# Sixteen small loads issued by GpSimd beside a saturated load queue

## The chip, the cores and the metric

The kernel runs on one core of a Trainium2 chip. The metric is the device time of one execution in microseconds; the time before is the median of two runs. The profile comes from one further look at one execution on the same program: its span goes from the first to the last instruction.

## The reference

One decode step of a transformer block for two sequences, in bfloat16. `_layernorm`, `_softmax` and the ReLU-gated feed-forward are the usual ones.

```python
# x (2, 1, 512); k_cache, v_cache (2, 32, 8192, 128); wq (512, 4096); wo (4096, 512)
q = (layernorm(x) @ wq)                       # 32 heads of 128
scores = einsum("bhqd,bhkd->bhqk", q, k) * 128 ** -0.5
o = einsum("bhqk,bhkd->bhqd", softmax(scores), v)
h = x + o @ wo
gate, up = layernorm(h) @ W_gate, layernorm(h) @ W_up      # 1376 wide
out = h + ((gate * (gate > 0)) * up) @ W_down
```

The two caches are 268 MB of the 281 MB that are read.

## The kernel before

The attention is done four heads at a time (`NH = 4`): 15 such steps, and the last four heads as two steps of two heads. A step needs a tile of K and a tile of V, each 128 partitions by 64 KB (8.39 MB). There are three buffers of that size, `bufs[0]` to `bufs[2]`. K of step i lies in `bufs[2 * i % 3]` and V in `bufs[(2 * i + 1) % 3]`: K0 in 0, V0 in 1, K1 in 2, V1 in 0, K2 in 1 and so on.

All big loads go through SP's queue (`load_tile`, L165), in the order in which they are written, and each is issued when what was in its buffer has been used. At the start SP issues W_q into the first half of `bufs[2]` (L193), then K0 and V0. ACT issues five loads of x, of one row each, into row 0 and 1 of `bufs[2]` (L190). The layer norm of x, the query projection (L252, L255) and the copies of the queries to `qrep` follow; then SP issues K1 into `bufs[2]` (L279), which is free once W_q, x and the queries in it are no longer needed.

```python
wq_sb = bufs[2][:, 0:HALF].rearrange("p (c n) -> p c n", c=KC)
qrow = bufs[2][0:B, HALF:HALF + Hq * Dh]
xr = bufs[2][0:B, HALF + Hq * Dh:HALF + Hq * Dh + D]
```

The rest of `bufs[2]` is used by nothing before K1 fills it.

In each step VectorE multiplies the K tile by the query (`products`, L375), adds the products up by halving (`scores`, L393, L395) and finds the maximum; a part of the tile goes through TensorE instead (`scores_pe`). ACT makes the exponentials (L415), VectorE places them (L420), and TensorE multiplies them with V (`values`, L446). V of the next step is issued after `scores`, K of the step after that after `values`.

GpSimd only fills constants at the start (L198 to L232, the last being `eps_col`), copies `qzp` (L281), which the two-head steps at the end read, and adds two rows near the end (L641, L642).

The order of the instructions on each engine is the written one (`manual_schedule`); the framework adds the semaphore waits. It counts DMAs that GpSimd issues on eight semaphores in turn, so that the ninth waits for the first to land before it is issued, and so on.

Of the kernel before, what the change touches and what calls it, by code (L numbers as in the profile page):

```python
# [13 lines left out]
def _free(t, offset, dims):  # L14

    return bass.AP(tensor=t.tensor, offset=t.offset + offset, ap=[t.ap[0]] + [list(d) for d in dims])


def _dram(t, offset, dims):
    return bass.AP(tensor=t.tensor, offset=t.offset + offset, ap=[list(d) for d in dims])  # L20
# [3 lines left out]
def kernel(  # L24
# [13 lines left out]
    nc = tc.nc  # L38
    P = nc.NUM_PARTITIONS
    B, Sq, D = A_x.shape  # L40
    _, Hkv, Sk, Dh = A_k_cache.shape
    Hq = A_wq.shape[1] // Dh
# [12 lines left out]
    HALF = TILE // 2  # L55
# [17 lines left out]
    FSETS = [(0, 5), (5 * P, 3), (8 * P, 1), (9 * P, 1), (F - P, 1)]  # L73
    FC = 11
    AGAIN = 32

    assert Sq == 1 and Hkv == Hq and Dh == P and D == KC * P and Hq == 32 and Sk == 8192 and B == 2
    assert F == 11 * P - AGAIN

# [12 lines left out]
    bufs = [big.tile([P, TILE], bf16, name=f"tile{k}") for k in range(3)]  # L92
# [94 lines left out]
    with tc.manual_schedule():  # L187

        for b, k, n in ((0, 0, 2), (0, 2, 2), (1, 0, 2), (1, 2, 1), (1, 3, 1)):
            nc.scalar.dma_start(  # L190
                out=xr[b:b + 1, k * P:(k + n) * P], in_=_dram(A_x, b * D + k * P, [[D, 1], [1, n * P]]),
# [10 lines left out]
            out=nscale, in_=nscale, compare_op=ALU.not_equal, fill=-SCALE,  # L202
# [5 lines left out]
            out=ident_f, in_=ident_f, compare_op=ALU.not_equal, fill=1.0,  # L208
# [4 lines left out]
            out=sel, in_=sel, compare_op=ALU.not_equal, fill=1.0,  # L213
# [9 lines left out]
            out=pick, in_=pick, compare_op=ALU.not_equal, fill=1.0,  # L223
# [7 lines left out]
            nc.gpsimd.memset(ownb[j * (P // NH):(j + 1) * (P // NH), j, :], 1.0)  # L231
        nc.gpsimd.memset(eps_col, EPS)  # L232
        nc.scalar.activation(out=warm, in_=eps_col, func=ACT.Sqrt)


        x_ps = ps.tile([P, KC, B], bf16, tag="mx")
# [11 lines left out]
        for g0 in range(0, NQ, 4):  # L248
            for n0 in range(NH * g0 * Dh, NH * (g0 + 4) * Dh, 4 * Dh):
                q_ps = ps2.tile([B, 4 * Dh], f32, tag="o")  # L250
                for c in range(KC):
                    nc.tensor.matmul(  # L252
                        out=q_ps, lhsT=xn[:, c, :], rhs=wq_sb[:, c, n0:n0 + 4 * Dh], start=(c == 0), stop=(c == KC - 1),
                    )
                nc.vector.tensor_copy(qrow[:, n0:n0 + 4 * Dh], q_ps)  # L255
            for b in range(B):
                r_ps = ps2.tile([P, 4, Dh], f32, tag="tp")
                for j in range(NH):
                    nc.tensor.matmul(
                        out=r_ps[j * (P // NH):(j + 1) * (P // NH)], lhsT=sel[:, b, 0:P // NH],  # L260
# [5 lines left out]
        for j in range(2):  # L266
            nc.tensor.matmul(
                out=r_ps[j * (P // 2):(j + 1) * (P // 2)], lhsT=sel[:, B - 1, :],
# [38 lines left out]
        def sums(i):  # L307

            _, _, n, z = heads(i)
            z_ps[i] = ps.tile([P, n], f32, tag="mx", name="z_ps")  # L310
            nc.tensor.matmul(out=z_ps[i], lhsT=ones, rhs=z, start=True, stop=True)
# [175 lines left out]
        def lay_rows(k, sps, scalar=False):  # L487

            r = SROWS[k]
            or_ps = ps.tile([P, B, r], f32, tag="mx")  # L490
            for b in range(B):
                nc.tensor.matmul(out=or_ps[:, b, :], lhsT=sps[b], rhs=rest[r], start=True, stop=True)
            if scalar:
                nc.scalar.activation(out=orow[k], in_=or_ps.rearrange("p b c -> p c b"), func=ACT.Copy)
            else:
                nc.vector.tensor_copy(orow[k], or_ps.rearrange("p b c -> p c b"))
# [77 lines left out]
        at = [0, 0]  # L574
# [12 lines left out]
        for k in range(1, len(SETS)):  # L587
# [3 lines left out]
            out=wo[:, (HM + 1) * D:Hq * D], in_=_dram(A_wo, (HM + 1) * Dh * D, [[P // 4 * D, 4], [D, P // 4], [1, D]]),  # L591
# [19 lines left out]
        for w, src in ((0, B_W_gate), (1, B_W_up)):  # L611
            nc.sync.dma_start(
                out=wgu[:, w].rearrange("p c f -> p (c f)"), in_=_dram(src, 0, [[KC * F, P], [1, KC * F]]),
            )
        for q0 in range(AGAIN, P, AGAIN):
            nc.sync.dma_start(
                out=wd_sb[q0:q0 + AGAIN, FC - 1, :], in_=_dram(B_W_down, (F - P + q0) * D, [[D, AGAIN], [1, D]]),
            )
        for f0, n in FSETS[:-1]:
# [10 lines left out]
            out=z2_ps, lhsT=ones, rhs=_free(zc, ((B - 1) * NQ + groups[Q][1]) * NH, [[1, nb]]), start=True, stop=True,  # L630
# [14 lines left out]
        for k in range(1, len(SETS)):  # L645
            lay_rows(k, sps[k - 1])
        nc.vector.memset(wd_sb[0:AGAIN, FC - 1, :], 0.0)
        sums(Q + 2)
# [45 lines left out]
        for c in range(KC):  # L694
            nc.tensor.transpose(hT_ps[:, c, :], hb[:, c].rearrange("p k b -> p (k b)"), ident)
        nc.scalar.activation(
            out=hrow.rearrange("q (p c) -> q p c", c=KC), in_=hT_ps.rearrange("q c p -> q p c"), func=ACT.Copy,
# [9 lines left out]
            out=gate, in0=g_ps, scalar=0.0, in1=_free(rvar, 0, [[0, FC], [1, B]]), op0=ALU.max, op1=ALU.mult,  # L707
# [59 lines left out]
```

## Time and profile before

| | before |
|---|---|
| median of the runs | 659.38 us (659.29 to 659.46, two runs) |
| span of the profiled execution | 657.5 us; the runs are 1.9 us longer than it |
| DMA | 281.37 MB, mean 428 GB/s |
| VectorE (DVE) busy | 558.1 us, 85% of the span |
| TensorE (PE) busy | 352.1 us, 54% |
| ScalarE (ACT) busy | 123.6 us, 19% |
| GpSimd (POOL) busy | 24.1 us, 4%, in 36 instructions |
| chain that ended last | DVE 42%, DMA 37%, PE 18% |

Busy shares are means over the span. The chain follows each piece of work back to what released it; its DMA pieces are waits for a tile to land. The DMA lines tell how much of the sixteen DMA engines' time each queue took: q1 is SP's queue, q10 is ACT's. The windows give the same numbers for a stretch of the span.

### The profile page before, as it was taken

To read this page: it belongs to the slowest core of one execution; us is meant where nothing else is said; L and a number is where in the kernel's file an instruction comes from. 1 tells how busy PE (TensorE), PEld (TensorE's weight loads), DVE (VectorE), ACT (ScalarE), POOL (GpSimd) and SP (SyncE) were. 2 spreads that over 40 slices of the span, in tenths; PEclk is the share of its full clock that TensorE was granted. 3 is DMA by queue.
4 is the path that set the end of the run, shared out by engine and by line. 5 is a ranking of instruction groups with operands and counts; after the bars stand their busy time and mean duration, and the time that the engine had idled before them with its cause. 6 is when DMAs were issued, how large, how long until landed. Compare 5 with 4: busy or idle time off the path is not lost.

```text
span 657.5 us, 5117 instructions
## 1 busy us (share of the span) xinstructions
PE 352.1 (54%) x2118; PEld 158.9 (24%) x2118; DVE 558.1 (85%) x252; ACT 123.6 (19%) x337; POOL 24.1 (4%) x36
## 2 busy tenths in 40 slices
PE   0730934809175380926539092552918458291997
PEld 0310311304022130312204031220403224030456
DVE  0599697988979799897979989796997969999982
ACT  0230030200203020030301103030210304201870
POOL 3080000000000000000000000000000000000020
PEclk9975775958778596877959687695968869686895
DMA  9999999999999999999999999999999999999997
GB/s 383 447 444 447 387 440 443 447 399 444 439 443 436 419 436 435 439 439 436 423 443 424 439 440 427 447 416 443 439 423 440 423 443 436 423 444 413 425 425 291
DMA packets 6948, 281.37 MB, mean 428 GB/s; under 512 B 809, under 2 KB 1422, under 8 KB 1934
## 3 DMA queue, kind: packets, MB, share of 16 engines
q1 hardware_dynamic: 6916, 281.06, 99.1%
q8 instruction: 16, 0.26, 0.1%
q14 instruction: 6, 0.05, 0.0%
q10 hardware_dynamic: 10, 0.00, 0.0%
HBM read 281.05 MB, written 0.00 MB: 427 GB/s over the span
## 4 chain that ended last, share of the span: by engine, by line
DVE 42%; DMA 37%; PE 18%; ACT 1%; issue 1%; ACTq 0%; SPq 0%; DVEq 0%
DMA tile<-in_A_k_cache_dram 30%; DVE tile L375 19%; DVE tile L393 18%; PE pv_ps L446 16%; DMA tile<-in_A_wo_dram 4%; DVE scol L395 2%; DMA tile<-in_A_x_dram 2%; DMA tile<-in_B_W_down_dram 1%; PE q_ps L252 1%; DVE pgq L420 1%; ACT ecol L415 1%; DVE pm L399 1%; DVE qrep L395 0%; DVE pm L410 0%; DVE hmax L412 0%
## 5 line engine op out<-in xcount | busy, mean ns | idle before, releaser
L446 PE MATMUL pv_ps<-tile,pgq 128*16 128x512 bf16 x960 | 244.3, 421 | 235.8 <-DVE pgq L420 223.2
L375 DVE TENSOR_TENSOR tile<-tile,qrep 128x29696 bf16<-128x29696 bf16 (+3 forms) x16 | 232.4, 14524 | 44.9 <-DMA tile<-in_A_k_cache_dram 44.9
L393 DVE TENSOR_TENSOR tile<-tile 128x14848 bf16<-128x14848 bf16 (+7 forms) x68 | 236.4, 3477 | 2.2
L446 PEld LDWEIGHTS <-pgq 128*16 128x16 bf16 x960 | 91.6, 97 | 378.1 <-DVE pgq L420 234.5
L451 ACT ACTIVATE pv<-pv_ps 16x512 f32<-16x512 f32 (+1 forms) x16 | 9.4, 589 | 243.7 <-PE pv_ps L446 243.6
L350 ACT ACTIVATE tile<-t_ps 128x1024 bf16<-128x1024 bf16 x53 | 52.6, 1022 | 12.6 <-PE t_ps L349 12.1
L415 ACT ACTIVATE ecol<-scol,nmax 128x256 bf16<-128x256 f32 x14 | 7.1, 508 | 196.1 <-DVE nmax L414 196.1
L340 PE MATMUL row_ps<-tile,qz 128*24 128x512 bf16 (+1 forms) x98 | 30.1, 389 | 18.0 <-ACT tile L350 17.9
L349 PE MATMUL t_ps<-ident,tile 128*128 128x128 bf16 x424 | 32.3, 229 | 13.0 <-DMA tile<-in_A_k_cache_dram 13.0
L349 PEld LDWEIGHTS <-tile 128*128 128x128 bf16 x424 | 25.8, 103 | 28.1 <-issue 14.2
L395 DVE TENSOR_REDUCE scol<-tile 128x232 f32<-128x1856 bf16 (+1 forms) x14 | 28.9, 2067 | 0.5
L641 POOL TENSOR_TENSOR tile<-ident 6x2 bf16<-6x2 bf16 x1 | 2.1, 2147 | 583.5 <-ACT tile L381 583.5
L420 DVE TENSOR_TENSOR pgq<-ecol,ownb 128x1024 bf16<-128x1024 bf16 x15 | 10.4, 692 | 10.3 <-ACT ecol L415 10.3
L381 ACT ACTIVATE tile<-tile 128x128 bf16<-128x128 bf16 x60 | 17.6, 293 | 1.9 <-DVE tile L375 1.9
L281 POOL COPY qzp<-qTs 128x4 bf16<-128x4 bf16 x1 | 15.0, 14982 | 26.1 <-DVE qTs L276 26.1
L375 DVE TENSOR_TENSOR tile<-tile,qpair 128x4096 bf16<-128x4096 bf16 (+3 forms) x4 | 15.5, 3883 | 0.0
L340 PEld LDWEIGHTS <-qz 128*24 128x24 bf16 (+1 forms) x98 | 7.9, 92 | 27.6 <-issue 22.7
L239 DVE CAST xc<-x_ps 128x8 f32<-128x8 bf16 x1 | 0.2, 167 | 15.5 <-PE x_ps L238 15.5
L367 ACT ACTIVATE scol<-sc_ps 32x24 f32<-32x24 f32 (+1 forms) x56 | 11.7, 209 | 7.7 <-PE sc_ps L362 7.2
L362 PE MATMUL sc_ps<-ident_f,tile 24*128 24x24 f32 (+2 forms) x68 | 7.2, 220 | 11.1 <-ACT tile L358 11.1
L358 ACT ACTIVATE tile<-row_ps 24x512 f32<-24x512 f32 (+2 forms) x17 | 10.0, 586 | 13.5 <-PE row_ps L340 13.5
L381 ACT ACTIVATION_READ_ACCUMULATOR tile<-tile 128x1 f32 x60 | 11.2, 186 | 0.0
(133 smaller groups left out, 143.8 us busy)
## 6 DMA issues: line engine op xcount, KB each, us to landing
tile<-in_A_k_cache_dram SPq DMA_DIRECT2D x2, 4096.0 KB
tile<-in_A_v_cache_dram SPq DMA_DIRECT2D x2, 4096.0 KB, 19.6
tile<-in_A_wq_dram SPq DMA_DIRECT2D x1, 4096.0 KB, 12.2
tile<-in_A_wo_dram SPq DMA_DIRECT2D x1, 2048.0 KB
tile<-in_B_W_gate_dram SPq DMA_DIRECT2D x1, 1376.0 KB, 22.8
tile<-in_B_W_up_dram SPq DMA_DIRECT2D x1, 1376.0 KB
tile<-in_A_wo_dram SPq DMA_DIRECT2D x1, 1024.0 KB, 23.8
tile<-in_B_W_down_dram SPq DMA_DIRECT2D x1, 640.0 KB
```

The source lines that it names most:

```text
L281: nc.gpsimd.tensor_copy(qzp[:, :, 6:8], qTs[:, B - 1, Hq - NH:Hq].rearrange("p (k j) -> p k j", j=2),)
L340: nc.tensor.matmul(out=row_ps, lhsT=z, rhs=s.kt[:, (nv + c0 + k) * Dh:(nv + c0 + k + 4) * Dh], start=(u == 0), stop=(u == U - 1),)
L349: nc.tensor.transpose(t_ps[:, k, :], s.kt[:, t * Dh:(t + 1) * Dh], ident)
L350: nc.scalar.activation(out=s.kt[:, (nv + c0) * Dh:(nv + c0 + TPC) * Dh], in_=t_ps.rearrange("p t s -> p (t s)"), func=ACT.Copy,)
L367: nc.scalar.activation(out=scols[s.i][r, nv:s.nt].rearrange("p (u t) -> p t u", t=4), in_=sc_ps[r, :, :, j], func=ACT.Copy,)
L375: nc.vector.tensor_tensor(out=kv, in0=kv, in1=_free(s.qr, 0, [[0, n], [1, Dh]]), op=ALU.mult)
L381: nc.scalar.activation(out=kv, in_=kv, func=ACT.Copy, accum_out=scols[s.i][:, t:t + 1])
L393: nc.vector.tensor_tensor(out=lo, in0=lo, in1=hi, op=ALU.add)
L395: nc.vector.tensor_reduce(out=scol[:, s.na:s.nv], in_=_free(s.kt, s.na * Dh, [[Dh, s.nv - s.na], [1, 8]]), axis=AXIS.X, op=ALU.add,)
L415: nc.scalar.activation(out=ecol, in_=scols[s.i], func=ACT.Exp, scale=SCALE, bias=nmax, accum_out=zs[:, s.b, s.g:s.g + 1],)
L420: nc.vector.tensor_tensor(out=s.pg, in0=_free(ecol, 0, [[VG, s.nt // VG], [0, NH], [1, VG]]), in1=_free(ownb, 0, [[0, s.nt // VG], [VG, NH ...
L446: nc.tensor.matmul(out=pv_ps[s.i][r, :], lhsT=s.pg[:, u].rearrange("p j t -> p (j t)"), rhs=s.vt[:, u * VG * Dh:(u + 1) * VG * Dh], start= ...
```

## The change

After its memsets GpSimd issues sixteen DMA loads. All read from the start of W_q; each goes to an own stretch of `bufs[2]`, behind x, in 1 to 100 partitions. Row lengths are odd numbers of two-byte elements (74 to 1018 bytes); the rows make 173 in all and 36,553 elements. What they write is read by nothing, and K1 is later loaded over it, so the framework makes the issue of K1 wait for all sixteen; the product on K1 and matmuls of a later step that read `bufs[2]` name their semaphores too. No other instruction is added, removed or moved on any engine.

```diff
+    EXTRA = [
+        (1, 509), (1, 503), (1, 499), (1, 491), (1, 487), (1, 479), (1, 467), (1, 463), (17, 461), (3, 457), (5, 449),
+        (7, 443), (19, 439), (13, 433), (100, 37), (1, 431),
+    ]
...
         nc.gpsimd.memset(eps_col, EPS)
         nc.scalar.activation(out=warm, in_=eps_col, func=ACT.Sqrt)
+        at = HALF + Hq * Dh + D
+        for rows, n in EXTRA:
+            nc.gpsimd.dma_start(out=bufs[2][0:rows, at:at + n], in_=_dram(A_wq, 0, [[Hq * Dh, rows], [1, n]]))
+            at += n + n % 2
```

## The prediction

> **What bounds the kernel now.** I read the page first, the DMA lines above all.
>
> ```profile
> span 657.5 us, 5117 instructions
> DMA packets 6948, 281.37 MB, mean 428 GB/s; under 512 B 809, under 2 KB 1422, under 8 KB 1934
> q1 hardware_dynamic: 6916, 281.06, 99.1%
> q10 hardware_dynamic: 10, 0.00, 0.0%
> ```
>
> One queue, q1 (SP's loads), keeps the sixteen DMA engines busy for 99.1% of the span. Next the windows, cut where tiles land (columns: PE, PEld, DVE, ACT, POOL busy, granted clock, DMA share, GB/s):
>
> ```profile
> 31.70:51.10 19.40, 6.73 (x53) 3.84 (x50) 18.95 (x4) 5.86 (x11) 14.98 (x1) 0.68 1.03 447
> 51.10:70.50 19.40, 3.46 (x9) 1.14 (x10) 14.75 (x10) 0.60 (x2) 0.00 (x0) 0.50 1.01 436
> ...
> 109.50:611.00 501.50, 270.62 (x1350) 115.26 (x1349) 449.91 (x158) 80.09 (x168) 0.00 (x0) 0.76 1.00 432
> ```
>
> The DMA share is 1.00 over 500 us, while VectorE, the busiest engine, works 450 of them. One 8.39 MB tile takes 19.3 us. So the end moves by whatever time the DMA engines stand still, and by nothing else as long as the others keep their slack. The third view is SP's own line, which shows when loads are handed over:
>
> ```profile
> 1.66 0.42 SPq L165 DMA_DIRECT2D tile<-in_A_v_cache_dram  x1
> 30.96 0.33 SPq L165 DMA_DIRECT2D tile<-in_A_k_cache_dram  x1
> 64.47 0.33 SPq L165 DMA_DIRECT2D tile<-in_A_v_cache_dram  x1
> 83.93 0.33 SPq L165 DMA_DIRECT2D tile<-in_A_k_cache_dram  x1
> ```
>
> The second line is K of step 1 (K1), which goes into the very buffer that the new loads write. It is issued at 30.96, but V of step 0 (V0) is still being moved then: K0 landed at 32.30, so V0 ends one tile later, at 51.1 to 51.6 on most DMA engines; K1 was complete at 72.48, less 19.4 gives 53.0 for the last one. K1's issue thus has about 20 us to spare.
>
> **What the change adds.** Nothing is removed or moved. Sixteen DMA issues stand on GpSimd's queue behind its last memset, and three kinds of wait come with them.
>
> *The issues themselves.* GpSimd reaches them at 6.46. The trace has no DMA issued by GpSimd. The nearest rows are SP's and ACT's issues (0.33 to 0.51 us) and GpSimd's slowest small operation (L641, 2.15 us): 5 to 34 us for sixteen. Behind them on GpSimd stands only the copy of qzp (L281), needed first at 614.89 (L340), so this time itself is covered. Without waits they end between 12 and 41.
>
> *The ninth to the sixteenth wait for the first to the eighth to land,* since there are eight semaphores. How long a small load needs to land beside q1 the trace shows on x, whose five loads are ten packets (five of data, five of completion) on q10:
>
> ```profile
> 2.11 12.96 DMA tile<-in_A_x_dram
> 15.07 0.14 issue
> 15.20 0.28 PE x_ps L238 x4
> ```
>
> 12.96 us for ten packets of at most 512 B is 1.3 us each. In the packet records they start at 6.54, 7.78, 8.99, 10.22, 11.44, 12.66 and so on, 1.21 apart, which is the time that a DMA engine takes for one 32 KB row of W_q; the last waited 2.42, one 64 KB row of K0. So a small packet waits for one whole row of q1 each time it is its queue's turn, data and completion each. From 12.4 on a turn costs 2.42 us (19.3 us for eight rows per engine).
>
> *SP's K1 issue waits for all sixteen.* Behind it in SP's order stand V1 and every later load. The sixteen loads are 173 rows (nine of one row, and 17, 3, 5, 7, 19, 13 and 100) and at least sixteen completions. Spread as evenly as can be, 173 / 16 is 11 data packets for an engine, and some completions: with one completion per load on each engine, 27 turns. Four fit before 12.4, and 23 more at 2.42 us last until 68. If all go to one engine, as x's did, it is longer still. But at 51.1 to 53.0 q1 runs empty, and then nothing stands between the small packets: they take 9 to 27 ns each, as x's did. So by this count K1 is released shortly after V0's last row, at about 53.2, whatever the split.
>
> *The bytes.* 36,553 elements are 73 KB: 0.17 us over all engines, 2.7 us if one engine moved them all; I take 0.3 where they add to the end, and nothing here, because the engines stand still for longer.
>
> *Waits on VectorE and TensorE.* The product on K1 and matmuls of a later step that read this buffer also name the new semaphores; SP has waited for them long before, so 0. SP's eight more waits at 17 ns are 0.14 us.
>
> **The sum.** The last packets at 53.0, 0.2 for what is left and for SP to see it, 1.1 to 1.4 from issue to first packet (W_q: issued at 0.74, first packet at 2.1; the output: issued at 655.56, packet at 656.68): K1 starts at about 54.6 on all engines, instead of 51.1 to 51.6 on most and 53.0 on one. That is 3.4 us of standstill on most, 1.6 on the late one; I take 3.0. Later loads don't give it back: V1 at 64.47 and K2 at 83.93 depend on work for step 0, which is not late, and from there the queue is never empty in either kernel. 657.5 + 3.0 = 660.5, and with the 1.9 us that lie between this span and the median of the runs, 662.4 us.
>
> **Rival 1: all hidden.** If a whole load takes one turn on each engine, its completion with its data, there are sixteen turns. Four before 12.4 and twelve at 2.42 end at 41.4, before 49.7 (V0's end less 1.4), and K1 is in the queue in time. What is left are the bytes: 659.4 + 0.3 = 659.7, up to 662. For it speaks that GpSimd's loads may be packed otherwise than ACT's; against it x's rows, where data and completion waited apart. The Trainium skill, page "DMA: Bandwidth & Descriptors", section "Queues, rings and completion order", says that an engine goes round the queues packet by packet and drains a packet of typically 9 to 17 descriptors before it switches. By that rule the sum would be this rival's; the trace agrees on the going round, but x's one-row loads show one descriptor at a time.
>
> **Rival 2: VectorE locks GpSimd out (the slower side).** These rows stand in the timeline:
>
> ```profile
> 32.41 15.08 DVE L375 TENSOR_TENSOR tile<-tile,qrep 128x28672 bf16<-128x28672 bf16 x1
> 32.56 14.98 POOL L281 COPY qzp<-qTs 128x4 bf16<-128x4 bf16 x1 [26.09 <-DVE qTs L276]
> ...
> 47.53 14.73 DVE L393 TENSOR_TENSOR tile<-tile 128x14336 bf16<-128x14336 bf16 x4
> 62.30 2.02 DVE L395 TENSOR_REDUCE scol<-tile 128x224 f32<-128x1792 bf16 x1
> ```
>
> A copy of 128x4 took 14.98 us because the product on VectorE had begun first; it ended with it. If writing a load's descriptors is held in the same way, each load not yet issued at 32.4 waits for a gap between VectorE's instructions: the first at 47.5, the next at about 55, 59, 61 and 62. One or two left cost nothing beyond the forecast to 5 us (K1 at 55.3, its first packet at 56.7, less 51.3), three to five 9 to 13, and with more than five K1 is issued after 64 and the price is 14: 673 to 674. It decides as soon as more than one load is unissued at 32.4. With a rotating engine the eighth load lands by 27 and nothing is left; if all go to one engine as x's did, the eighth lands at about 41 and the last two are left. The same price follows without a lock if GpSimd takes over 3.5 us for a load, above my bound. The Trainium skill, page "SBUF — State Buffer", section "Who interferes with whom", says that a two-input VectorE instruction holds up GpSimd's reads of SBUF, not its writes; the copy above reads, so its row agrees, and by this rule descriptors would pass and this rival falls back to the forecast.
>
> **Rival 3: faster.** The engines move a 64 KB row in 2.42 us throughout, back to back; nothing here makes rows shorter. Only a realignment of the late engine could give back some tenths.
>
> **How the numbers follow.** Forecast (K1 held to V0's end, 661 to 664): 0.52. All hidden (659.2 to 661): 0.22. Held up by VectorE within 13 us (665 to 672): 0.10; by more: 0.14. Faster by over 2%: 0.02. Two per cent, about what a measurement of this kernel can tell from no change, is 13.2 us: faster 0.02, within 0.84, slower 0.14. The range goes from the hidden case, 659.2, to 673, and leaves out the dearest lock and the gain.
>
> **What would show it.** Right: SP's second K issue moves from 30.96 to 53 to 54; a dip in GB/s at 51 to 55; K1's product on VectorE starts near 74 instead of 72.48; every later SP issue about 2 to 3 us late; the new GpSimd queue's packets strung out until 51 and ending in a burst. Wrong: K1's issue before 49 (rival 1), or after 55 with GpSimd's issues standing at the ends of VectorE's instructions (rival 2), or SP's later issues not shifted by what was lost at 51.

## The result, and the profile after

The changed kernel takes 666.0 us (665.85 to 666.14, two runs), the kernel before 659.38 us: a ratio of 1.0101, with a 95% interval of 1.0085 to 1.0117. It is 6.6 us slower. The forecast was 662.4 us. The direction, the place and the kind of loss were as forecast, but the loss is more than double the 3.0 us of the forecast. The profiled execution has a span of 664.3 us, 6.8 more than before.

The page of the kernel after, DMA lines (queue, kind: packets, MB, share of sixteen engines):

```profile
span 664.3 us, 5146 instructions
DMA packets 7461, 281.45 MB, mean 424 GB/s; under 512 B 1251, under 2 KB 1934, under 8 KB 2446
...
q1 hardware_dynamic: 6916, 281.06, 98.2%
...
q0 software_dynamic: 512, 0.07, 0.1%
...
q10 hardware_dynamic: 10, 0.00, 0.0%
```

q1 carries the same 6916 packets, but its share falls from 99.1% to 98.2%: the engines stood still, they hardly worked more. The new queue q0 holds 512 packets. That is sixteen loads times sixteen engines times two, although nine of the loads have only one row. The windows of the kernel after, cut as in the prediction (same columns):

```profile
31.70:51.10 19.40, 6.09 (x62) 3.85 (x61) 17.96 (x4) 6.60 (x13) 5.86 (x4) 0.74 0.96 414
51.10:70.50 19.40, 2.47 (x6) 0.79 (x7) 15.73 (x10) 0.60 (x2) 0.00 (x0) 0.50 0.80 326
109.50:611.00 501.50, 266.70 (x1336) 113.69 (x1336) 448.28 (x157) 78.08 (x159) 0.00 (x0) 0.76 1.00 433
```

The loss lies in the second window, where the DMA share falls from 1.01 to 0.80. (The first window's fall from 1.03 to 0.96 is part of the same loss: a row counts whole at its start, and in the kernel before most of K1's first rows started just ahead of 51.10.) Over the 500 us that follow it is 1.00, as before, so nothing is given back and little is added. SP's line in the timeline of the kernel after:

```profile
1.66 0.42 SPq L171 DMA_DIRECT2D tile<-in_A_v_cache_dram  x1
55.06 0.33 SPq L171 DMA_DIRECT2D tile<-in_A_k_cache_dram  x1
65.45 0.33 SPq L171 DMA_DIRECT2D tile<-in_A_v_cache_dram  x1
83.87 0.33 SPq L171 DMA_DIRECT2D tile<-in_A_k_cache_dram  x1
110.96 0.33 SPq L171 DMA_DIRECT2D tile<-in_A_v_cache_dram  x1
...
661.72 0.32 SPq L746 DMA_DIRECT2D out_dram<-tile  x1
```

K1 is issued at 55.06 instead of 30.96. V1 and K2, which wait for work of step 0, move little (65.45 against 64.47, 83.87 against 83.93); the next V is 5.3 us late (110.96 against 105.64), and the output at the end 6.16 (661.72 against 655.56). The two lines of the kernel before:

```profile
105.64 0.33 SPq L165 DMA_DIRECT2D tile<-in_A_v_cache_dram  x1
...
655.56 0.32 SPq L736 DMA_DIRECT2D out_dram<-tile  x1
```

The chain of waits of the kernel after around this place (start, us, what) tells why:

```profile
43.74 10.86 DMA tile<-in_A_wq_dram
54.60 0.02 issue
54.62 0.03 SPq L171
...
55.02 0.04 issue
55.06 22.14 DMA tile<-in_A_k_cache_dram
```

The last small load was issued at 43.74 and landed at 54.60; SP then went through its waits until 55.06. GpSimd's line in the timeline, with VectorE's product on K0 from its own line in the second fence, shows how it came to 43.74:

```profile
6.43 4.27 POOL L242 DMA_DIRECT2D tile<-in_A_wq_dram  x8
13.27 0.53 POOL L242 DMA_DIRECT2D tile<-in_A_wq_dram  x1 [2.57 <-DMA tile<-in_A_wq_dram]
15.70 0.51 POOL L242 DMA_DIRECT2D tile<-in_A_wq_dram  x1 [1.90 <-DMA tile<-in_A_wq_dram]
20.53 0.52 POOL L242 DMA_DIRECT2D tile<-in_A_wq_dram  x1 [4.33 <-DMA tile<-in_A_wq_dram]
25.37 0.52 POOL L242 DMA_DIRECT2D tile<-in_A_wq_dram  x1 [4.32 <-DMA tile<-in_A_wq_dram]
30.21 0.53 POOL L242 DMA_DIRECT2D tile<-in_A_wq_dram  x1 [4.32 <-DMA tile<-in_A_wq_dram]
32.85 0.51 POOL L242 DMA_DIRECT2D tile<-in_A_wq_dram  x1 [2.11 <-DMA tile<-in_A_wq_dram]
37.49 0.57 POOL L242 DMA_DIRECT2D tile<-in_A_wq_dram  x1 [4.13 <-DMA tile<-in_A_wq_dram]
43.74 0.52 POOL L242 DMA_DIRECT2D tile<-in_A_wq_dram  x1 [5.68 <-DMA tile<-in_A_wq_dram]
44.26 4.27 POOL L291 COPY qzp<-qTs 128x4 bf16<-128x4 bf16 x1
```

```profile
33.40 15.08 DVE L385 TENSOR_TENSOR tile<-tile,qrep 128x28672 bf16<-128x28672 bf16 x1
```

An issue takes 0.53 us (505 to 682 ns each), and eight go out in 4.27 us. From the ninth on, GpSimd waits for an earlier load (the idle time in brackets). From 15.70 to 30.21 these loads land 4.84 us apart: twice the 2.42 us of a 64 KB row. The steps from 13.27 to 15.70 and from 30.21 to 32.85 are only about one row long. They fall where W_q and K0 end; in the packet records q1 then has a 4-byte packet of its own between two rows, and a small packet that goes in turn with it waits 9 ns instead of a row.

**Where the 6.8 us are.** The packet and semaphore records of the two traces give the rest. V0's last rows end at 51.0 to 51.5 on fifteen engines and at 52.9 on the late one (before: 50.8 to 51.2, and 52.7). The last small packet goes through at 53.01, but on each engine the completions of the small loads come one by one, some 0.17 us apart. On fifteen engines the last one is in by 53.62. On the late engine, which was busy with V0 longest, they run from 53.37 to 54.60, the end of the chain's wait; so that one engine sets the release of K1. K1's first packets come at 56.01 to 56.89, 1.0 to 1.8 us after its issue. Before, K1's rows followed V0's without a gap; the mean start of the sixteen first rows moves from 51.11 to 56.21, by 5.1 us. These first rows take 3.12 us on average instead of 2.42: 0.7 more. 5.1 and 0.7 make the 5.8 us by which K1's rows end later on the first engine (75.96 against 70.16), and the tiles behind it end 5.4 to 5.9 later there throughout. The program's end takes 2.6 us from the output's issue (661.72 to 664.28) where it took 2.0 (655.56 to 657.54): 0.6 more. That is 6.4 of the 6.8; some tenths at the end of the kernel remain unassigned.

### The profile page after: what moved, and what is told of

Read it like the earlier page. It is cut to its first block, busy times and chain, and to the rows that moved or that the text cites. A ratio compares the mean times of both kernels' runs of the same rounds, so it can differ in the third digit from the quotient of the medians.

```text
span 664.3 us, 5146 instructions
## 1 busy us (share of the span) xinstructions
PE 349.6 (53%) x2118; PEld 157.8 (24%) x2118; DVE 558.1 (84%) x252; ACT 123.7 (19%) x337; POOL 21.7 (3%) x52
## 3 DMA queue, kind: packets, MB, share of 16 engines
q1 hardware_dynamic: 6916, 281.06, 98.2%
## 4 chain that ended last, share of the span: by engine, by line
DVE 42%; DMA 39%; PE 16%; POOL 1%; issue 1%; ACT 1%; SPq 0%; DVEq 0%; ACTq 0%; POOLq 0%
DMA tile<-in_A_k_cache_dram 27%; DVE tile L385 19%; DVE tile L403 18%; PE pv_ps L456 16%; DMA tile<-in_A_wq_dram 7%; DMA tile<-in_A_wo_dram 4%; DVE scol L405 2%; DMA tile<-in_B_W_down_dram 2%; DVE pgq L430 1%; ACT ecol L425 1%; POOL tile L242 1%; DVE pm L409 1%; DVE qrep L405 0%; DVE pm L420 0%; DVE hmax L422 0%
## 5 line engine op out<-in xcount | busy, mean ns | idle before, releaser
L359 PE MATMUL t_ps<-ident,tile 128*128 128x128 bf16 x424 | 31.3, 224 | 13.7 <-DMA tile<-in_A_k_cache_dram 13.7
L262 PE MATMUL q_ps<-tile,xn 128*2 128x512 bf16 x32 | 9.9, 477 | 1.0 <-DVE xn L191 1.0
## 6 DMA issues: line engine op xcount, KB each, us to landing
tile<-in_A_wq_dram SPq DMA_DIRECT2D x1, 4096.0 KB, 12.4
```

Of the source, the lines that this page charges most:

```text
L359: nc.tensor.transpose(t_ps[:, k, :], s.kt[:, t * Dh:(t + 1) * Dh], ident)
```

## The experiments

The diffs are against the kernel after, unless said otherwise. What a run costs is its median less that of the kernel before, measured beside it (659.23 to 659.26 us). Two short names are used below: "the hold" is K1's late issue, "one-row" and "many-row" are the loads of `EXTRA`.

**The hold taken away.** The same number of loads goes to a tile of its own that K1 doesn't use. The loads keep their row numbers, but each row has one element.

```diff
+    apart = consts.tile([P, sum(n + n % 2 for _, n in EXTRA)], bf16)
-            nc.gpsimd.dma_start(out=bufs[2][0:rows, at:at + n], ...
+            nc.gpsimd.dma_start(out=apart[0:rows, at:at + n], ...
```

> The sixteen loads go into a tile of their own, cut to one element per row (the free memory holds no more) with the same numbers of rows, so K1's issue names none of them. Theory A (the time is lost because K1's issue is held until the last small load has landed, and 0.6 us at the program's end where GpSimd drains): K1 issued at 31, 659.4 + 0.6 + at most 0.3 = 660.0 to 660.4. Theory B (the small packets and GpSimd's queue themselves slow the big loads): about 666 as with the change, K1's issue at 31 or not.

K1 is issued where it was before:

```profile
30.87 0.33 SPq L170 DMA_DIRECT2D tile<-in_A_k_cache_dram  x1
```

661.32 us (660.59 to 663.02), ratio 1.0033 (1.002 to 1.0047). The hold is thus about 4.6 of the 6.6 us; 2.1 us (661.32 against 659.26) stay, more than expected. The next run has all sixteen loads with a single element, in the same tile:

```diff
-    EXTRA = [(1, 1), ... (17, 1), (3, 1), (5, 1), (7, 1), (19, 1), (13, 1), (100, 1), (1, 1)]
+    EXTRA = [(1, 1)] * 16
```

> As the kernel with the loads in a tile of their own, but sixteen loads of one element each: 512 small packets and 32 turns again, no loads of many rows. If the 2 us that are left there come from many short rows beside the big ones: 659.3 + 0.6 = 659.9 to 660.3. If from the completions or from GpSimd's queue: 661.3 again.

```profile
31.55 0.33 SPq L170 DMA_DIRECT2D tile<-in_A_k_cache_dram  x1
...
655.40 0.32 SPq L745 DMA_DIRECT2D out_dram<-tile  x1
```

659.83 us (659.73 to 660.49), ratio 1.001 (1.0001 to 1.0019): 0.6 us. Its tiles land within some tenths of before (K1 at 70.21 on the first engine against 70.16), and its output goes out earlier than before (655.40 against 655.56), yet its span is 0.4 us longer. So 0.6 us of the price of sixteen loads is at the program's end, and sixteen one-row loads that nobody waits for cost the rest of the kernel nothing. The other 1.5 us of the first run came with rows, not with the hold. (Beside the run with sixteen one-row loads into `bufs[2]` below, 665.54 us, this run gives the hold alone: 5.7 us. The two also differ in the length of the rows.)

**How many loads it takes.** Eight, nine and ten loads of the list:

```diff
-    EXTRA = [... sixteen ...]
+    EXTRA = [(1, 509), (1, 503), (1, 499), (1, 491), (1, 487), (1, 479), (1, 467), (1, 463)]   # nine: and (17, 461)
+                                                                                               # ten: and (3, 457)
```

> Only the first eight loads, all of one row, into the same place. Theory A, with two turns on every DMA engine for each load whatever its rows: sixteen turns, the last load lands at 43.4, K1 is issued at about 43.9 and the engines never run empty: 660.0 to 660.4. Theory B: half the small packets, half the loss, about 662.7. Theory C (the prediction's count: one turn for each row and each completion): nothing held either, 660.

> The first nine loads. Theory A: eighteen turns, the last ends at about 48.5, K1 is issued at about 49 and its first row comes at 50, just before V0's last row ends: nothing stands still, 0.6 us from the program's end, 659.9 to 660.5. With ten it was 663.9. A loss in proportion to the number of loads: 663.

> The first ten loads of the change. Theory A (two turns per load beside SP's rows, K1 held until the last has landed): twenty turns, sixteen of them by 43.3, four more at 2.42 are not done when V0 ends, so K1 is held to V0's end as with sixteen, but six completions fewer are left then at 0.17 us each: K1 issued at about 53.8 instead of 55.06, 664.5 to 665.2. Were the loss in proportion to the number of loads: 659.4 + 10/16 of 6.6 = 663.5.

SP's issue of K1 in the timelines of eight, nine and ten loads, in this order:

```profile
43.77 0.33 SPq L168 DMA_DIRECT2D tile<-in_A_k_cache_dram  x1
```

```profile
48.25 0.33 SPq L168 DMA_DIRECT2D tile<-in_A_k_cache_dram  x1
```

```profile
53.11 0.33 SPq L168 DMA_DIRECT2D tile<-in_A_k_cache_dram  x1
```

| loads | K1 issued | median | ratio (interval) |
|---|---|---|---|
| eight | 43.77 | 659.89 (659.38 to 660.90) | 1.0011 (1.0001 to 1.0020) |
| nine | 48.25 | 660.25 (659.67 to 661.26) | 1.0016 (1.0006 to 1.0025) |
| ten | 53.11 | 663.88 (663.42 to 664.24) | 1.0072 (1.0055 to 1.0089) |
| sixteen | 55.06 | 666.00 (665.85 to 666.14) | 1.0101 (1.0085 to 1.0117) |

The ninth and the tenth load each move K1's issue by 4.5 to 4.9 us: two turns of 2.42. Nine loads end at 48.25, which leaves K1 the 1.0 to 1.8 us that it needs before V0 ends at 51, and cost 1.0 us. Ten end at 53.11, after V0 on most engines, and cost 4.6. From there on the loads only drain, and six more cost 1.95 us of issue time and 2.0 of run time. Nine came out within the expected range, eight 0.1 us and ten 0.6 us under it. The range for nine counted on 0.6 us at the program's end, and that was wrong: the spans of these three runs end 2.05 to 2.06 us after the output's issue, about as in the kernel before (1.98) and not as with sixteen loads (2.56). What the 0.6 us of eight loads are is open.

**Whether the rows count.** All sixteen loads with one row each, into `bufs[2]`:

```diff
-        (1, 463), (17, 461), (3, 457), (5, 449), (7, 443), (19, 439), (13, 433), (100, 37), (1, 431),
+        (1, 463), (1, 461), (1, 457), (1, 449), (1, 443), (1, 439), (1, 433), (1, 37), (1, 431),
```

> Sixteen loads of the change's lengths, but of one row each, into the same place. Theory A with two turns per load whatever its rows: K1 held to the same point, issued at 54.8 to 55.1, 665.4 to 666.0. Were rows what holds K1 (theory C, on rotating engines): sixteen loads of one row are some seventeen turns, K1 issued at about 46, 660.

```profile
54.61 0.33 SPq L168 DMA_DIRECT2D tile<-in_A_k_cache_dram  x1
```

665.54 us (665.26 to 665.93), ratio 1.0096 (1.0081 to 1.0111). The hold is the same with 16 rows as with 173, so turns go by loads, not by rows. K1's issue is 0.45 us earlier; the medians are 0.46 apart, but their intervals overlap, so that the rows' bytes cost anything here is not shown. Eight loads with many rows, all among the first eight:

```diff
-    EXTRA = [... sixteen ...]
+    EXTRA = [(17, 461), (3, 457), (5, 449), (7, 443), (19, 439), (13, 433), (100, 37), (17, 463)]
```

> Eight loads again, but those of many rows (17, 3, 5, 7, 19, 13, 100 and 17: 181 rows in all). Theory A with two turns per load: as with eight loads of one row, K1 issued at about 43.9, 660.0 to 660.4. Theory C (a turn for each row): 181 rows over 16 engines are 11 turns and more besides the completions, which reaches V0's end: K1 issued at 53 to 54, 663 to 665. Theory B: about 662.7.

```profile
46.17 0.33 SPq L168 DMA_DIRECT2D tile<-in_A_k_cache_dram  x1
```

662.04 us (661.55 to 663.35), ratio 1.0046 (1.0031 to 1.0061). K1 is issued in time, yet it costs 2.2 us more than eight one-row loads. In the packet records the fourteen 518-byte packets of the load with 100 rows (seven rows each) take 486 ns on average beside the big rows, against 28 ns in the kernel after, where they went through after V0's end. Two more runs have eight loads of 100 short rows, and eight of 19 long ones:

```diff
-    EXTRA = [... sixteen ...]
+    EXTRA = [(100, 37)] * 8        # the other: [(19, 439)] * 8
```

> Eight loads of 100 rows of 74 bytes each, into the same place: sixteen turns, so K1 is not held to V0's end (issued by 49). In the kernel with eight loads of many rows the fourteen 518-byte packets of the one such load took 0.49 us each beside the big rows, against 0.03 alone. If they are what cost 2 us there, eight such loads cost several times that: 664 to 672. If the cost lies elsewhere: 660 to 662.

> Eight loads of 19 rows of 878 bytes each, into the same place: sixteen turns, K1 issued by about 46. Their 1756-byte packets took 0.31 us beside the big rows, against 0.07 alone: 8 x 0.24 = 1.9 us for an engine that carries one of each load, so 661 to 662; if only the load of 100 rows costs: 660.

661.98 us (661.18 to 663.45), ratio 1.0046 (1.0031 to 1.0061), and 662.52 us (661.54 to 663.44), ratio 1.0052 (1.0034 to 1.0070). The windows of the 100-row and the 19-row kernel over the first 30 us end in GB/s; the kernel before has 420 there:

```profile
0.00:30.00 30.00, 11.95 (x48) 4.49 (x48) 7.65 (x22) 4.35 (x7) 9.95 (x41) 1.00 0.97 388
```

```profile
0.00:30.00 30.00, 11.42 (x45) 4.37 (x46) 6.98 (x22) 4.35 (x7) 9.50 (x41) 1.00 0.97 387
```

A window counts each 64 KB row whole at its start, so its GB/s jump when rows slip past its edge; the packet records are finer. K0's last rows end at 32.4 to 34.1 in the first and at 33.0 to 33.7 in the second, against 31.3 to 31.9 before: 1.0 to 2.2 us later, so most of the loss is there. It does not go by the number of slow small packets, as I had thought: with eight times as many of the 518-byte packets it is the same, and in the 19-row kernel the small packets are quick (77 ns), while the 64 KB rows of q1 take 2.57 us on average between 11 and 46 us (2.42 before). Loads with many rows disturb the big rows by about 2 us in all; what in them does it stays open.

**The big rows made shorter.** A turn lasts as long as the other queue's row. K0 and V0 are loaded in four pieces each, with rows of 16 KB; first in the kernel before alone, then in the kernel after.

```diff
-        load_tile(A_k_cache, steps[0], steps[0].kt)
-        load_tile(A_v_cache, steps[0], steps[0].vt)
+        load_tile(A_k_cache, steps[0], steps[0].kt, 4)
+        load_tile(A_v_cache, steps[0], steps[0].vt, 4)
```

> The kernel before, with K0 and V0 each cut into four loads with rows of 16 KB instead of 64 KB; no small loads. It is the base for the next kernel: 659 to 660 if short rows move as fast, as the same bytes go through the same engines.

> All sixteen small loads and K1 held by them, as in the change, beside K0 and V0 in rows of 16 KB. Theory A: a turn lasts one row of SP's queue, so 0.6 us instead of 2.42 after W_q; 32 turns end at 12.4 + 28 x 0.6 = 29 to 31, K1 is issued at 31 to 33 and nothing stands still: 0.6 to 1.5 us over the same kernel without small loads, about 660.5. If a turn does not depend on the row of the other queue: K1 at 53 to 55 and 666.

The first costs nothing that can be told from noise: 659.52 us (659.05 to 659.94), ratio 1.0005 (0.9996 to 1.0015). The timeline of the second, SP's issue of K1 and GpSimd's last issue:

```profile
32.43 0.33 SPq L171 DMA_DIRECT2D tile<-in_A_k_cache_dram  x1
```

```profile
20.91 0.52 POOL L242 DMA_DIRECT2D tile<-in_A_wq_dram  x1 [0.65 <-DMA tile<-in_A_wq_dram]
```

GpSimd's sixteenth issue comes at 20.91 instead of 43.74, and K1's at 32.43 instead of 55.06. 662.63 us (662.14 to 662.94), ratio 1.0053 (1.0038 to 1.0068). K1 still waits for the last load, which lands at 32.29, but that is long before V0 ends, so the hold costs nothing with all sixteen loads and all 173 rows in place. K1's issue came as expected (31 to 33). The expected 660.5 was missed by 2.1 us: now the many-row loads run beside the big rows (518-byte packets 642 ns on average), which fits the price of the runs above; one-row loads beside the 16 KB rows were not run, so this part is not shown.

**K1 in two halves.** The first half goes over W_q alone, which no small load touches, and so needs no wait for them:

```diff
-        load_tile(A_k_cache, steps[1], steps[1].kt)
+        load_tile(A_k_cache, steps[1], steps[1].kt, 2)
```

> All sixteen loads as in the change; K1's load is cut into two loads of 64 KB and 64 KB halves of each row (two of 4.2 MB), the first of which goes over W_q alone and names none of the small loads. Theory A: first half issued at about 29 to 31, second at 55; the first half keeps the engines busy from 51 to 61, nothing stands still: 659.4 + 0.6 + up to 0.5 = 660.0 to 660.6. Theory B: 666.

A miss: 665.61 us (664.93 to 665.77), ratio 1.0095 (1.0078 to 1.0112). SP's two issues in the timeline, and the window behind them (before: DMA share 0.97, 419 GB/s):

```profile
29.51 34.43 SPq L171 DMA_DIRECT2D tile<-in_A_k_cache_dram  x2
```

```profile
60.00:70.00 10.00, 2.34 (x6) 0.78 (x7) 6.54 (x8) 0.60 (x2) 0.00 (x0) 0.50 0.63 240
```

The first half is issued at 29.51, the second ends its issue at 63.94. I had taken 55 us as the time at which the small loads land. But it is the time at which q1 runs dry; with the first half behind V0 it runs dry half a tile later, near 61. The small loads keep waiting two turns each until then (by the semaphore records the eleventh to the thirteenth land at 54.18, 56.61 and 59.04, 2.4 apart, twice the 1.21 us of a 32 KB row), and the same hold comes there: the last lands at 63.29.

## Why the prediction was wrong in size

- **The bound** was right. The DMA share of the long window is 1.00 in both kernels, and the end moved by what the engines stood still, with no part given back.
- **The turns** were right in length and wrong in what makes them. I counted 173 rows and their completions, 27 turns per engine. The 512 packets of q0 and the staircase of eight, nine and ten loads say two turns per load on every engine, whatever its rows: 32 turns. The rows that an engine moves for one load go as one packet (518 bytes are seven rows of 74), so what x's one-row loads showed did not carry over to many rows. The first small packet came at 10.95, 4.5 us after the first issue, so four turns before 12.4 was too many. The Trainium skill, page "DMA: Bandwidth & Descriptors", section "Why a DMA increments its semaphore by 16 and not by 1", says that a DMA issued by GpSimd posts its completion on all sixteen engines whatever its shape; the 512 packets agree. Both counts run past V0's end, so the forecast of a hold did not suffer. Sixteen turns, as in rival 1, would have ended before it; the hold excludes that.
- **The step that failed is the drain after V0's end**: "The last packets at 53.0, 0.2 for what is left and for SP to see it". The last packet came at 53.01, as said, with some luck: the late engine's last row ended at 52.7 before, not at 53.0, and ends at 52.9 now. But the prediction took the packets' own 9 to 27 ns as the price of a load once q1 is empty. A load costs some 0.17 us between completions; what was left took until 54.60 on the late engine, and SP's waits, put at 0.14 us, until 55.06. The 0.2 us were 2.05. K1's release at 53.2 is what ten loads give (53.11), not sixteen.
- **Issue to first packet**, 1.1 to 1.4 us, was misread and came near all the same. The prediction's packet times are some 0.37 us later than the timeline's clock: on that clock x's packets start at 6.17, 7.40 and 8.62, V0's rows end at 50.8 to 51.2 and 52.7, and W_q's first packet and the output's came 1.04 and 0.75 us after their issue. K1's came after 1.0 to 1.8. It starts at 56.0 to 56.9, not at 54.6.
- **The standstill** I put at 3.4 us on most engines and at 1.6 on the late one, and took 3.0. K1's first rows start 5.1 later on average, and the whole kernel follows those; the late engine gives nothing back.
- **Left out**: 0.7 us by which the first rows after the hole are slower, and 0.6 us at the program's end, which the run with sixteen single elements shows alone. So 3.0 forecast, 2.1 more of standstill, 0.7 and 0.6 make the 6.4 us accounted for.
- **GpSimd's issues**, 5 to 34 us for sixteen, took 8.5, and the copy of `qzp` had its cover (it ended at 48.5, needed after 610). VectorE's further waits stand ahead of its product on K1 for 0.6 us (77.19 to 77.80 in the chain); the sum's 0 held for the end because the next load that depends on this product, V of step 2, is still issued (110.96) before K2 has been moved (its rows end from 114.63 on).
- **Rival 2** fell. The issues at 37.49 and 43.74 lie inside VectorE's product (33.40 to 48.48) and took 0.57 and 0.52 us, while the copy beside them was again held until the product's end (44.26 to 48.53). The rule of the Trainium skill, page "SBUF — State Buffer", section "Who interferes with whom", by which GpSimd's reads are held up and its writes are not, agrees with these three rows; that an issue only writes SBUF is not shown by them.

## What to carry to other kernels

Here small loads from GpSimd beside a saturated queue waited in turns: about two for each load, each as long as a row of the other queue. Where a large load has to wait for such small ones, compare the last one's landing with the moment at which the big queue runs dry. If it falls before, the wait costs little (nine loads, 1.0 us); if it falls after, everything behind the waiting issue stands still, and the hole costs the drain, the waits, the issue and a slow restart together (ten loads, 4.6). In these runs shorter big rows took the hold away, loading half of K1 ahead of the waiting issue only moved it, and none of the versions here is faster than the kernel without the small loads.

## What the runs showed of the hardware

- A GpSimd load uses two packets on all sixteen engines even for one element: 512 packets for sixteen loads, with 4-byte packets where an engine has no data. Beside 64 KB rows its landing comes 4.84 us after the one before, beside 16 KB rows 1.24.
- With nothing else to move, such loads complete 0.15 to 0.19 us apart on each engine, though their packets take 9 to 73 ns (kernel after, and sixteen one-row loads).
- After the hole, the first 64 KB row of an engine takes 3.12 us on average instead of 2.42 (2.97 with sixteen one-row loads, 3.07 with ten loads).
- With sixteen GpSimd loads the span ends 2.5 to 3.0 us after the output's issue, in the kernel before after 1.98, and with eight to ten loads after 2.05 to 2.06. Why was not separated.
- Eight loads of many rows beside the big rows cost about 2 us that eight one-row loads do not (662.0 and 662.5 against 659.89), and slow q1's rows from 2.42 to 2.57 us in one case. The cause was not separated.
